# One 128-row product for the output of the later chunks of a gated linear attention with a mixing layer

## The chip, the cores and the metric

The kernel runs on one core of a Trainium2 chip. The metric is the device time of one execution in microseconds; the figure of a kernel is the median of its runs.

## What is computed

A gated linear attention over 4 batches of 8 heads, 768 positions and 48 channels a head, and behind it a mixing layer over the 384 joined channels. Everything is fp32. The change lies in the attention.

```
# attention
f = 1 / (1 + exp(-f_logit))
for t in range(S):
    state = f[:, :, t, :, None] * state + einsum('bhd,bhe->bhde', k[:, :, t], v[:, :, t])
    y[:, :, t] = einsum('bhd,bhde->bhe', q[:, :, t], state)
# mixing layer, x = y with its heads joined
theta = x @ w_theta
zr, zi = x * cos(theta), x * sin(theta)
u = x + einsum('ts,bsd->btd', w_tok_r, zr) + einsum('ts,bsd->btd', w_tok_i, zi)
out = u + max(u @ w_ch, 0)
```

## The kernel before

The positions of a batch are cut into 6 chunks of 128 (`NC`), so there are 24 chunks, `m` from 0 to 23. Heads are held in 4 pairs (`NP`): in a tile of q, k or f, rows 0 to 47 are the channels of the pair's first head and rows 64 to 111 those of its second, the columns are the pair and the position. The gates of a chunk are summed along the positions (`gate_sum`, a scan against the `carry` tile of ones and zeros), and q and k are scaled with their exponentials, so that within a chunk the attention is a masked product of q and k, and what came before is a state of 48x48 for each head.

A chunk is worked on in halves of 64 positions (`HALVES`, `t`), and `j` counts the two heads of a pair. Its steps:

- `sc` (`att_scores`): 16 matmuls make the key-value products of each half and head (line 312), and 16 the scores of the half against itself (line 318). Two of the four PSUM banks `a` receive them, one for each `j`. In the last chunk of a batch the second half's key-value products are left out.
- `sa` and `st` (`att_mid`, `att_new`) on VectorE add the products to the state: `mid` is the state at the chunk's middle, `st` at its end. `sm` fades it.
- `ma` (`att_mask`): two operations on VectorE multiply the scores with the `causal` triangle.
- `oa` (`att_old`, line 395): 16 matmuls of q with the state: the old state for the first half (none in the first chunk of a batch, so 8 matmuls there), `mid` for the second.
- `ob` (`att_own`, line 406): 16 matmuls of the masked scores with v, added to those of `oa` in PSUM.
- `xc` copies the result out, and the mixing layer takes it on.

All of these matmuls have at most 64 rows and 64 columns of weights. Scores of the pair's second head are written to the rows of the other half (`rows(j, t)`), and v is loaded with a second, rolled copy of the odd heads, so that the four matmuls of a group fall on the four different 64x64 tiles of the array. An fp32 matmul shows as two instructions in the trace.

The mixing layer runs on full 128x128 tiles with 384 columns: `th` (angles, 9 instructions), `f` (the products over positions, line 531, 6 instructions a step, or 4 in the first batch), `c` (the channel product, line 549, 9 a step). `tn`, `se`, `ab`, `tr`, `ro`, `zh`, `zl`, `v`, `uh`, `ul`, `cv` and `so` are its steps on the other engines. `fl` (line 583) is one product with a single column that sums up a flag.

There is no scheduler: `ORDER` is a table of some 1,200 step names, each calls its function once with the next number, and every engine runs its instructions in the order in which the steps stand there. A name after a slash sends a step to another engine (`/D` VectorE, `/A` ScalarE, `/P` GpSimd). `wu` steps at the start keep TensorE working on the `carry` tile while the first loads arrive. All loads are issued by SyncE, in that order, and each waits there until its buffer is free: `lf`, `lk`, `lq`, `lv` (line 600, two buffers) and `lw` for the weights.

Of the kernel before, what the change touches and what calls it, by code (L numbers as in the profile page):

```python
# [8 lines left out]
F32 = mybir.dt.float32  # L9
F32R = mybir.dt.float32r  # L10
I32 = mybir.dt.int32
U16 = mybir.dt.uint16
F16 = mybir.dt.float16
BF16 = mybir.dt.bfloat16
AF = mybir.ActivationFunctionType
ALU = mybir.AluOpType
# [6 lines left out]
P = 128  # L23
# [20 lines left out]
FULL = 1  # L44

CUT = 0
KB, XB = 10, 12
BL = 32

# [3 lines left out]


ORDER = (
# [36 lines left out]
)  # L92


# [1 line left out]
def gla_moe_kernel(  # L96
# [4 lines left out]
    f: bass.AP,  # L101
    v: bass.AP,
    vt: bass.AP,
    w_theta: bass.AP,
    w_r: bass.AP,
    w_i: bass.AP,
# [11 lines left out]

    carry = const.tile([P, NP, C], F32, tag="carry", name="carry")
    nc.vector.memset(carry, 1.0)
    nc.vector.memset(carry[:, :, 0:1], 0.0)

    causal = const.tile([P, C // 2], F32, tag="causal", name="causal")
    nc.gpsimd.memset(causal, 1.0)
# [143 lines left out]
    pss, scs, psks, kts, pkvs, mids, states, pys, xs, pxts = ({} for _ in range(10))  # L270
    HALVES = [(t, slice(64 * t, 64 * t + 64)) for t in range(2)]

    def rows(j, t):

        return HALVES[j ^ t][1]
# [28 lines left out]
    def att_scores(m):  # L304
        kt, qt = loaded["k", m], loaded["q", m]
        pss[m] = [bank([P, NP, C], f"pss{m}{j}", 1) for j in range(2)]
        pkvs[m] = [t[:, :, 64:64 + D] for t in pss[m]]
        for p in range(NP):
            for j, r in HALVES:
                h, c = 2 * p + j, slice(64 * j, 64 * j + D)  # L310
                for t, ts in HALVES[:1 if last_chunk(m) else 2]:
                    nc.tensor.matmul(pkvs[m][t][c, p, :], kts[m][ts, p, c], vs[m][ts, h * D:(h + 1) * D],  # L312
                                     start=True, stop=True)
        for p in range(NP):
            for t, ts in HALVES:
                for j in range(2):
                    r = slice(64 * j, 64 * j + D)
                    nc.tensor.matmul(pss[m][j][rows(j, t), p, :64], kt[r, p, ts], qt[r, p, ts], start=True, stop=True)  # L318

    def att_mask(m):  # L320
        t = sb.tile([P, 2, NP, C // 2], F32, tag="sc", bufs=2, name=f"sc{m}")
        scs[m] = [t[:, j] for j in range(2)]
        for j in range(2):
            masked = nc.vector.tensor_tensor(scs[m][j], pss[m][j][:, :, :64],  # L324
                                             causal.unsqueeze(1).to_broadcast([P, NP, 64]), op=ALU.mult)
            if not j:
                after(masked, old_done[m])
# [3 lines left out]
    def warm_up(n):  # L331

        if n < 4:
            nc.tensor.matmul(banks[n], carry[:, 0, :], carry.rearrange("p n t -> p (n t)"), start=True, stop=True)
            return
        nc.tensor.matmul(warm, carry[:, 0, :], carry[:, 1, :], start=True, stop=True)

    def att_keys(m):
        psks[m] = bank([P, NP, C], f"psk{m}", 1)
# [256 lines left out]
        return go  # L596

    def load_v(m):
        vs[m] = sb.tile([P, DM + NP * D], F32, tag="v", bufs=2, name=f"v{m}")
        nc.sync.dma_start(vs[m], v[m // NC, m % NC])  # L600

# [15 lines left out]
    def group(fn):  # L617
# [13 lines left out]
        "e4": lambda n: split_hi(NCH + n), "e5": lambda n: split_lo(NCH + n),  # L631
        "wu": warm_up, "gp": gate_end, "sa": att_mid,
        "sc": att_scores, "ma": att_mask, "ke": att_keys, "kt": att_ktok,
        "xb": x_turn, "xw": x_store, "xr": x_load,
        "kb": keys_turn, "ks": keys_store, "kl": keys_load,
        "st": inner(att_new), "sm": inner(att_fade), "oa": att_old, "ob": att_own, "xc": att_x, "xt": att_turn, "xs": keep_x,
# [101 lines left out]
def layout(inputs):  # L738
    import numpy as np

    def rows(a):
        t = np.asarray(a).transpose(0, 1, 3, 2).reshape(B, NP, 2, D, S)
        t = np.concatenate([t, t[:, :, :, :64 - D]], axis=3).reshape(B, NP, P, NC, C)
        return np.ascontiguousarray(t.transpose(0, 3, 2, 1, 4))

    v = np.asarray(inputs["v"])
    vc = v.transpose(0, 2, 1, 3).reshape(B, NC, C, NP, 2, D)
    odd = np.roll(vc[:, :, :, :, 1], C // 2, axis=2).reshape(B, NC, C, NP * D)
    vt = v.transpose(0, 1, 3, 2).reshape(B, NP, 2, D, S)
    vt = np.concatenate([vt, vt[:, :, :, :64 - D]], axis=3).reshape(B, NP, P, S)  # L750
    return {
# [2 lines left out]
        "f": rows(inputs["f_logit"]),  # L754
        "v": np.concatenate([vc.reshape(B, NC, C, DM), odd], axis=3),
        "vt": np.ascontiguousarray(vt),
        "w_theta": np.ascontiguousarray(inputs["moe_w_theta"]).view(np.int64),
        "w_r": np.ascontiguousarray(np.asarray(inputs["moe_w_tok_r"]).T).view(np.int64),
        "w_i": np.ascontiguousarray(np.asarray(inputs["moe_w_tok_i"]).T).view(np.int64),
# [22 lines left out]
```

## Time and profile before

| what | value |
|---|---|
| runs | 323.01, 324.25, 328.32 us; median 324.25 |
| the profiled execution's own time | 321.26 us |
| its span in the profile | 319.5 us |
| TensorE busy | 308.1 us (96%) |
| VectorE busy | 248.5 us (78%) |
| ScalarE busy | 194.6 us (61%) |
| GpSimd busy | 59.3 us (19%) |
| granted clock of TensorE | 1.0 |

The profile is of one execution. Matmuls are pipelined and overlap, and their ends are modelled, so the time from one matmul's start to the next says more than its duration. PE is TensorE, PEld its weight loads, DVE is VectorE, ACT ScalarE, POOL GpSimd, SP SyncE. The part of the span around the first 10 us is spent on the first loads and gates, while TensorE runs its warm-up products.

### The profile page before, as it was taken

To read this page: it belongs to the slowest core of one execution; us is meant where nothing else is said; L and a number is where in the kernel's file an instruction comes from. 1 tells how busy PE (TensorE), PEld (TensorE's weight loads), DVE (VectorE), ACT (ScalarE), POOL (GpSimd) and SP (SyncE) were. 2 spreads that over 40 slices of the span, in tenths; PEclk is the share of its full clock that TensorE was granted. 3 is DMA by queue.
4 is the path that set the end of the run, shared out by engine and by line. 5 is a ranking of instruction groups with operands and counts; after the bars stand their busy time and mean duration, and the time that the engine had idled before them with its cause. 6 is when DMAs were issued, how large, how long until landed. Compare 5 with 4: busy or idle time off the path is not lost.

```text
span 319.5 us, 10259 instructions
## 1 busy us (share of the span) xinstructions
PE 308.1 (96%) x4314; PEld 279.5 (87%) x4314; DVE 248.5 (78%) x449; ACT 194.6 (61%) x346; POOL 59.3 (19%) x74
## 2 busy tenths in 40 slices
PE   7889999999999999999999999999999999999993
PEld 4767677668999999998999999998999999999993
DVE  3999998999999999988968789789637476652122
ACT  6899897999998998885248670875151333111000
POOL 3124123354044520211030102103200000000000
PEclk9999999999999999999999999999999999999999
DMA  7999889974327685868778787955661431100002
GB/s 229 397 313 399 322 248 345 339 253 124 114 34 207 203 212 137 220 164 215 175 177 209 191 205 215 224 113 149 148 149 41 107 69 33 49 27 25 25 28 79
DMA packets 82610, 55.23 MB, mean 173 GB/s; under 512 B 51584, under 2 KB 66432, under 8 KB 82560
## 3 DMA queue, kind: packets, MB, share of 16 engines
q1 hardware_dynamic: 82416, 54.34, 58.8%
q8 instruction: 35, 0.57, 0.8%
q10 hardware_dynamic: 144, 0.20, 0.2%
q14 instruction: 15, 0.12, 0.1%
HBM read 43.77 MB, written 10.75 MB: 171 GB/s over the span
## 4 chain that ended last, share of the span: by engine, by line
PE 77%; DMA 11%; DVE 4%; ACT 3%; SPq 2%; issue 1%; DVEq 0%; ACTq 0%
PE pm L531 43%; PE pch L549 11%; PE a L475 9%; PE a L406 3%; DMA v<-in_v_dram 3%; PE a L395 3%; DMA ut<-xd 3%; PE a L318 3%; PE a L312 2%; DMA raw<-in_w_i_dram 2%; DMA out_dram<-ut 2%; DMA k<-in_k_dram 2%; PE a L341 1%; PE a L419 1%; SPq L595 1%
## 5 line engine op out<-in xcount | busy, mean ns | idle before, releaser
L531 PE MATMUL pm<-wp,z 128*128 128x384 f32 x756 | 142.4, 339 | 0.0
L531 PEld LDWEIGHTS pm<-wp,z 128*128 128x128 f32 x756 | 131.1, 188 | 1.0
L549 PE MATMUL pch<-uhl,wch 128*128 128x384 f32 x216 | 41.2, 338 | 0.0
L549 PEld LDWEIGHTS pch<-uhl,wch 128*128 128x128 f32 x216 | 37.5, 188 | 0.4
L260 POOL TENSOR_TENSOR q<-q,p 128x512 f32<-128x512 f32 x15 | 22.2, 1478 | 54.0 <-DMA q<-in_q_dram 37.8
L245 DVE TENSOR_TENSOR_SCAN f<-carry,f 128x512 f32<-128x512 f32 x24 | 29.1, 1211 | 3.5 <-ACT f L241 3.4
L475 PE MATMUL a<-wth,xh 128*128 128x384 f32 x144 | 30.1, 344 | 0.9 <-ACT ktok L149 0.3
L149 ACT CAST uhl<-ut 128x384 fp32r<-128x384 f32 x18 | 9.2, 511 | 31.5 <-DVE ut L535 31.5
L475 PEld LDWEIGHTS a<-wth,xh 128*128 128x128 f32 x144 | 24.7, 188 | 2.2 <-ACT xh L149 0.6
L531 PE MATMUL pm<-value,zf 128*128 128x384 f32 x72 | 25.3, 495 | 0.0
L563 DVE SCALAR_TENSOR_TENSOR ut<-pch,ut 128x384 f32<-128x384 f32 x24 | 13.1, 549 | 14.8 <-PE pch L549 14.8
L381 POOL TENSOR_TENSOR st<-st,pes 128x192 f32<-128x192 f32 x17 | 11.0, 645 | 71.3 <-DVE st L377 71.3
L265 DVE SCALAR_TENSOR_TENSOR k<-f,k 128x512 f32<-128x512 f32 x24 | 17.5, 729 | 5.4 <-ACT f L253 4.0
L324 DVE TENSOR_TENSOR sc<-a,causal 128x256 f32<-128x256 f32 x48 | 17.9, 415 | 3.9 <-PE a L395 3.7
L508 DVE TENSOR_TENSOR w<-w,x 128x768 f32<-128x768 f32 x18 | 17.1, 949 | 4.8 <-ACT w L501 4.8
L406 PEld LDWEIGHTS a<-v,sc 64*64 64x64 f32 x768 | 15.0, 134 | 5.8 <-issue 1.7
L240 ACT ACTIVATE f<-f 128x512 f32<-128x512 f32 x24 | 15.1, 629 | 7.4 <-DMA f<-in_f_dram 7.4
L531 PEld LDWEIGHTS pm<-value,zf 128*128 128x128 f32 x72 | 13.0, 190 | 7.5
L500 ACT ACTIVATE w<-w 128x384 f32<-128x384 f32 x24 | 12.6, 524 | 11.2 <-DVE w L495 10.9
L515 DVE TENSOR_TENSOR z<-w,z 128x768 fp32r<-128x768 f32 x18 | 18.2, 1010 | 1.5 <-ACT z L149 1.4
L252 ACT ACTIVATE p<-f 128x512 f32<-128x512 f32 x24 | 15.2, 632 | 6.7 <-POOL q L260 4.6
L535 DVE TENSOR_TENSOR ut<-pm,ut 128x384 f32<-128x384 f32 x24 | 13.1, 550 | 7.4 <-PE pm L531 7.3
(92 smaller groups left out, 527.5 us busy)
## 6 DMA issues: line engine op xcount, KB each, us to landing
v<-in_v_dram SPq DMA_DIRECT2D x24, 288.0 KB, 4.4
f<-in_f_dram SPq DMA_DIRECT2D x24, 256.0 KB, 4.1
q<-in_q_dram SPq DMA_DIRECT2D x24, 256.0 KB, 4.4
k<-in_k_dram SPq DMA_DIRECT2D x24, 256.0 KB, 4.7
raw<-in_w_r_dram SPq DMA_DIRECT2D x12, 383.8 KB, 5.9
raw<-in_w_i_dram SPq DMA_DIRECT2D x12, 383.8 KB, 6.5
out_dram<-ut SPq DMA_DIRECT2D x23, 192.0 KB, 2.5
kd<-kt SPq DMA_DIRECT2D x56, 64.0 KB, 2.8
```

The costliest lines, as they stand in the source:

```text
L240: nc.scalar.activation(ft, ft, AF.Exp, scale=-1.0, accum_out=odds[:, col:col + 1])
L245: nc.vector.tensor_tensor_scan(fl, carry[:, pairs(h)].rearrange("p n t -> p (n t)"), fl, 0.0, ALU.mult, ALU.add)
L252: nc.scalar.activation(ps_[m][:, pairs(h)], ft, AF.Exp, scale=-1.0)
L260: on(nc.vector).tensor_tensor(qt, qt, ps_[m][:, pairs(h)], op=ALU.mult)
L265: nc.vector.scalar_tensor_tensor(kt, loaded["f", m][:, pairs(h)], E_TOP, kt, op0=ALU.min, op1=ALU.mult)
L324: masked = nc.vector.tensor_tensor(scs[m][j], pss[m][j][:, :, :64], causal.unsqueeze(1).to_broadcast([P, NP, 64]), op=ALU.mult)
L406: nc.tensor.matmul(pys[m][j][ts, p, :], l, r, start=(old[t] is None and p == 0), stop=(p == NP - 1))
L475: nc.tensor.matmul(pths[m], l, r, start=(n == 0), stop=(n == len(ms) - 1))
L508: nc.vector.tensor_tensor(zfs[m] if full else w, w, xs[m].unsqueeze(1).to_broadcast([P, 2, DM]), op=ALU.mult)
L515: nc.vector.tensor_tensor(zs[m][:, 0], zfs.get(m, ws.get(m)), zs[m][:, 1], op=ALU.subtract)
L531: nc.tensor.matmul(pms[g, d], l, r, start=(s == 0 and i == 0), stop=(s == NC - 1 and i == len(ms) - 1))
L549: nc.tensor.matmul(pcs[g, d], l, r, start=(es[0] == 0 and n == 0), stop=(es[-1] == KD - 1 and n == len(ms) - 1))
```

## The change

From chunk 12 on (`KC = 12`), `oa` and `ob` are one step `oc` (`att_both`). For one half and one head the weights of its matmul hold, over 128 rows, the masked scores (64 rows) and q (48 rows at the other 64), and the moving operand holds v and, in the same rows as q, the state. Where 16 rows are left between, `v`'s tile has zeros from a new input `vh`. For it:

- `lv` loads two pieces into a `v` tile of two halves; the rolled copy of the odd heads is no longer used there.
- `qc` (`join_q`) copies q into the two `join` tiles on ScalarE, four copies a chunk, two where there is no old state.
- `m0` and `m1` (`join_old`, `join_mid`) copy the old and the middle state into the `v` tile on ScalarE, two copies each.
- `ma` writes the masked scores into the join tiles with four operations over 64 rows.
- the scores of both heads are written to the rows of their own half.
- the join tiles take the two buffers that the masked scores of two chunks had.

A chunk without an old state (12 and 18) has `k = 64` rows in the first half's product, one with it 112, and the second half's always 128. The tile shape goes by the rows: 64x64 for 64 rows, 128x64 for 112 and 128.

`carry` holds bytes now, and the warm-up products read a tile of ones instead. `ORDER` is written anew for all chunks: as many `f`, `th` and `c` steps, but other places, and other engines for some (`tn/D` 7 times, was 12; `xs/D` 3, was 8; `xc/D` 13, was 6; `gq/P` 17, was 15; `d5/P` 4, was 6; `uh/D` 8, was 6).

```diff
+U8 = mybir.dt.uint8
+KC = 12
 ORDER = (
-    "tr se so kb lf sm/P ab/A cv ks tr oa gp v gq/P sc ma ul f lq sa so ge ro ob cv oa zh ro so f lq xc",
+    "se c st m1 ro sm/P xh xs xl oc zh gk sc lv qc gs f lk xc kl kb ge lf th zl ks gp cv m0 d5/P ma ab/A",
...
-    carry = const.tile([P, NP, C], F32, tag="carry", name="carry")
-    nc.vector.memset(carry, 1.0)
-    nc.vector.memset(carry[:, :, 0:1], 0.0)
+    some = sb.tile([P, DM], F32, tag="x", bufs=3, name="some")
+    nc.vector.memset(some, 1.0)
+    carry = const.tile([P, NP, C], U8, tag="carry", name="carry")
+    nc.vector.memset(carry, 1)
+    nc.vector.memset(carry[:, :, 0:1], 0)
...
+    def v_half(m, t):
+        return vs[m][HALVES[t][1], t, :] if m >= KC else vs[m][HALVES[t][1], :DM]
...
                 for j in range(2):
                     r = slice(64 * j, 64 * j + D)
-                    nc.tensor.matmul(pss[m][j][rows(j, t), p, :64], kt[r, p, ts], qt[r, p, ts], start=True, stop=True)
+                    out_rows = ts if m >= KC else rows(j, t)
+                    nc.tensor.matmul(pss[m][j][out_rows, p, :64], kt[r, p, ts], qt[r, p, ts], start=True, stop=True)
+
+    joins = {}
+
+    def join_q(n):
+        m = KC + n
+        joins[m] = [sb.tile([P, NP, 2, 64], F32, tag="sc", bufs=2, name=f"join{m}{t}") for t in range(2)]
+        for t, ts in HALVES:
+            if t or m % NC:
+                w = 64 if t else D
+                for j in range(2):
+                    a, b = 64 - 64 * t, 64 * j
+                    nc.scalar.copy(joins[m][t][a:a + w, :, j, :], loaded["q", m][b:b + w, :, ts])
+
+    def join_state(m, t, state):
+        st = vs[m][:, t, :].rearrange("q (p j d) -> q p j d", p=NP, j=2)
+        for j in range(2):
+            a, b = 64 - 64 * t, 64 * j
+            nc.scalar.copy(st[a:a + D, :, j, :], state[b:b + D])
+
+    def join_mid(n):
+        join_state(KC + n, 1, mids[KC + n])
+
+    def join_old(n):
+        m = KC + n // (NC - 1) * NC + n % (NC - 1) + 1
+        join_state(m, 0, states[m - 1])
+
+    def att_both(n):
+        m = KC + n
+        pys[m] = pkvs[m]
+        for p in range(NP):
+            for j in range(2):
+                for t, ts in HALVES:
+                    k = P if t else 64 + D if m % NC else 64
+                    h = 2 * p + j
+                    nc.tensor.matmul(pys[m][j][ts, p, :], joins[m][t][:k, p, j, :], vs[m][:k, t, h * D:(h + 1) * D],
+                                     start=True, stop=True)
 
     def att_mask(m):
+        if m >= KC:
+            for j in range(2):
+                for t, ts in HALVES:
+                    nc.vector.tensor_tensor(joins[m][t][ts, :, j, :], pss[m][j][ts, :, :64],
+                                            causal[ts].unsqueeze(1).to_broadcast([64, NP, 64]), op=ALU.mult)
+            return
...
     def load_v(m):
+        if m >= KC:
+            vs[m] = sb.tile([P, 2, DM], F32, tag="v", bufs=2, name=f"v{m}")
+            for r, src in ((slice(0, 64), slice(0, 64)), (slice(D, P), slice(64, P + 64 - D))):
+                nc.sync.dma_start(vs[m][r, r.start // D, :], vh[m // NC, m % NC, src])
+            return
```

What TensorE runs at the end of chunk 12. Names are tiles with their numbers: `sc12` are masked scores, `v12` the values, `a0` to `a3` the PSUM banks, `pch` the channel product `c`. Before, behind the scores of chunk 13:

```order
L318 MATMUL a2_94<-q13_1831,k13_1711 64x64
L406 MATMUL a1_93<-v12_1926,sc12_2222 64x48 x2
L406 MATMUL a0_92<-v12_1926,sc12_2222 64x48 x2
L406 MATMUL a1_93<-v12_1926,sc12_2222 64x48 x2
L406 MATMUL a0_92<-v12_1926,sc12_2222 64x48 x2
L549 MATMUL pch12_2245<-uhl10_1723,wch1_87 128x384
```

Of the change, behind a channel product and ahead of the key-value products of chunk 13 (line 321); `join120` is chunk 12's first half, `join121` its second:

```order
L602 MATMUL pch11_2116<-uhl12_2038,wch1_89 128x384
L363 MATMUL a0_94<-v12_1880,join120_1956 64x48
L363 MATMUL a0_94<-v12_1880,join121_1957 64x48
L363 MATMUL a1_95<-v12_1880,join120_1956 64x48
L363 MATMUL a1_95<-v12_1880,join121_1957 64x48
L321 MATMUL a2_96<-v13_1969,ktok13_2056 48x48
```

The product of chunk 12 has moved from behind the scores of chunk 13 to ahead of its key-value products; both fences leave out rows of the same pattern (there are eight rows of `L406` and sixteen of `L363`), and the first half and the second now alternate.

What VectorE runs around the masks of chunk 12. Before, they stand far behind the state of the chunk; the rows from its middle state to its end state:

```order
L371 COPY mid12_2072<-a1_93 128x192
L508 TENSOR_TENSOR w9_1964<-w9_1964,x9_1688 128x768
L377 TENSOR_TENSOR st12_2094<-a0_92,mid12_2072 128x192
L149 CAST z9_2096<-w9_1964 128x768
```

Of the change, the four masks come ahead of the middle state:

```order
L370 TENSOR_TENSOR join120_1956<-a0_94,causal_72 64x4x64
L370 TENSOR_TENSOR join121_1957<-a0_94,causal_72 64x4x64
L370 TENSOR_TENSOR join120_1956<-a1_95,causal_72 64x4x64
L370 TENSOR_TENSOR join121_1957<-a1_95,causal_72 64x4x64
L424 COPY mid12_2102<-a0_94 128x192
L616 SCALAR_TENSOR_TENSOR ut1_742<-pch10_2076,ut1_742 128x384
L535 TENSOR_SCALAR w10_2109<-a2_96 128x384
L540 SCALAR_TENSOR_TENSOR w10_2109<-w10_2109,a2_96 128x384
L430 TENSOR_TENSOR st12_2126<-a1_95,mid12_2102 128x192
```

The masks have become four rows of 64 partitions and have moved ahead of `mid12`.

## Rows read from the trace of the kernel before

**Rows 1.** The page: busy time of each engine, and 40 equal slices.
```profile
PE 308.1 (96%) x4314; PEld 279.5 (87%) x4314; DVE 248.5 (78%) x449; ACT 194.6 (61%) x346; POOL 59.3 (19%) x74
DVE  3999998999999999988968789789637476652122
PEclk9999999999999999999999999999999999999999
```
**Rows 2.** Busy time by stretch; columns as the second row names them.
```profile
core 0: us, PE busy (x) PEld busy (x) DVE busy (x) ACT busy (x) POOL busy (x), PEclk, DMA share, GB/s
60.00:120.00 60.00, 59.87 (x894) 52.49 (x893) 58.86 (x98) 57.21 (x103) 23.71 (x20) 1.00 0.59 172
120.00:260.00 140.00, 138.77 (x2136) 132.35 (x2134) 111.89 (x212) 76.01 (x134) 18.24 (x25) 1.00 0.66 163
```
**Rows 3.** Waits of TensorE: who for whom, us in total, times, longest.
```profile
PE a L334 <- DVE carry L123: 1.8, 1, 1.8
PE a L312 <- issue: 0.8, 1, 0.8
```
**Rows 4.** Groups of instructions on TensorE, by shape: busy us, mean ns.
```profile
L406 PE MATMUL a<-v,sc 64*64 64x48 f32 x768 | 18.2, 222 | 0.0
L395 PE MATMUL a<-mid,q 48*64 48x48 f32 x384 | 15.9, 221 | 0.0
```
**Rows 5.** Timeline of TensorE, 178 to 187 us: start, us, instruction, count.
```profile
178.54 0.47 PE L312 MATMUL a<-v,ktok 64*48 64x48 f32 x13
178.82 0.27 PE L318 MATMUL a<-q,k 48*64 48x64 f32 x1
...
179.49 5.48 PE L531 MATMUL pm<-wp,z 128*128 128x384 f32 x30
184.90 0.68 PE L406 MATMUL a<-v,sc 64*64 64x48 f32 x32
185.40 0.22 PE L395 MATMUL a<-st,q 48*64 48x48 f32 x1
```
**Rows 6.** The same timeline, the end of that block.
```profile
185.97 4.44 PE L531 MATMUL pm<-wp,z 128*128 128x384 f32 x24
```
**Rows 7.** Timeline of TensorE, chunk 16's scores.
```profile
168.50 0.55 PE L312 MATMUL a<-v,ktok 64*48 64x48 f32 x32
168.87 0.67 PE L318 MATMUL a<-q,k 48*64 48x64 f32 x32
```
**Rows 8.** Timeline of TensorE, `oa` of chunk 12 and what follows it.
```profile
135.46 0.49 PE L395 MATMUL a<-mid,q 48*64 48x48 f32 x10
135.74 0.25 PE L312 MATMUL a<-v,ktok 64*48 64x48 f32 x2
```
**Rows 9.** Timeline of TensorE around the flag's product.
```profile
225.62 0.69 PE L475 MATMUL a<-wth,xl 128*128 128x384 f32 x3
226.23 0.19 PE L583 MATMUL a<-worst,pair 128*1 128x1 f32 x2
226.35 1.83 PE L549 MATMUL pch<-uhl,wch 128*128 128x384 f32 x9
228.03 1.23 PE L531 MATMUL pm<-wp,z 128*128 128x384 f32 x6
```
**Rows 10.** Timeline of TensorE, a long run of `f` steps.
```profile
283.16 7.46 PE L531 MATMUL pm<-wp,z 128*128 128x384 f32 x42
290.46 1.73 PE L549 MATMUL pch<-uhl,wch 128*128 128x384 f32 x9
```
**Rows 11.** Groups on VectorE and ScalarE, by shape: busy us, mean ns, idle before.
```profile
L149 ACT COPY x<-a 128x192 f32<-128x192 f32 x36 | 9.7, 319 | 6.4 <-PE a L406 6.2 <-DVE w L508 0.2
L324 DVE TENSOR_TENSOR sc<-a,causal 128x256 f32<-128x256 f32 x48 | 17.9, 415 | 3.9 <-PE a L395 3.7
L373 DVE TENSOR_TENSOR mid<-a,st 128x192 f32<-128x192 f32 x20 | 7.0, 349 | 2.9 <-PE a L318 2.6
L482 DVE TENSOR_SCALAR w<-a 128x384 f32<-128x384 f32 x12 | 6.6, 548 | 1.8 <-PE a L475 1.6
L149 DVE COPY ut<-a 128x384 f32<-128x384 f32 x8 | 4.4, 547 | 0.0
L149 DVE COPY x<-a 128x192 f32<-128x192 f32 x12 | 3.7, 351 | 1.0 <-PE a L406 1.0
```
**Rows 12.** Waits of the DMA queue on SyncE, the `v` loads.
```profile
SPq L600 <- PE a L406: 14.4, 8, 3.5
```
**Rows 13.** The `v` loads' line: ns of an issue, minimum, median, maximum.
```profile
L600 SPq DMA_DIRECT2D v<-in_v_dram x24: 327/384/1011, 4.2 to 249.0; - x24
```

More of the change, by code (lines that the diff above doesn't have):

```diff
@@ L103, in gla_moe_kernel @@
     vt: bass.AP,
+    vh: bass.AP,
     w_theta: bass.AP,
@@ L311, in att_scores @@
                 for t, ts in HALVES[:1 if last_chunk(m) else 2]:
-                    nc.tensor.matmul(pkvs[m][t][c, p, :], kts[m][ts, p, c], vs[m][ts, h * D:(h + 1) * D],
+                    nc.tensor.matmul(pkvs[m][t][c, p, :], kts[m][ts, p, c], v_half(m, t)[:, h * D:(h + 1) * D],
                                      start=True, stop=True)
@@ L333, in warm_up @@
         if n < 4:
-            nc.tensor.matmul(banks[n], carry[:, 0, :], carry.rearrange("p n t -> p (n t)"), start=True, stop=True)
+            nc.tensor.matmul(banks[n].rearrange("p (n t) -> p n t", n=NP), some[:, :C],
+                             some[:, :C].unsqueeze(1).to_broadcast([P, NP, C]), start=True, stop=True)
             return
-        nc.tensor.matmul(warm, carry[:, 0, :], carry[:, 1, :], start=True, stop=True)
+        nc.tensor.matmul(warm, some[:, :C], some[:, C:2 * C], start=True, stop=True)
     def att_keys(m):
@@ L633, in gla_moe_kernel @@
         "sc": att_scores, "ma": att_mask, "ke": att_keys, "kt": att_ktok,
+        "qc": join_q, "m0": join_old, "m1": join_mid, "oc": att_both,
         "xb": x_turn, "xw": x_store, "xr": x_load,
@@ L748, in layout @@
     odd = np.roll(vc[:, :, :, :, 1], C // 2, axis=2).reshape(B, NC, C, NP * D)
+    vr = vc.reshape(B, NC, C, DM)
     vt = v.transpose(0, 1, 3, 2).reshape(B, NP, 2, D, S)
@@ L756, in layout @@
         "vt": np.ascontiguousarray(vt),
+        "vh": np.concatenate([vr[:, :, :C // 2], np.zeros_like(vr[:, :, :64 - D]), vr[:, :, C // 2:]], axis=2),
         "w_theta": np.ascontiguousarray(inputs["moe_w_theta"]).view(np.int64),
```

71 rows, old and new, of the table ORDER are left out of this document.

## The prediction

> **What bounds the kernel now.** First the page's busy times and slices [rows 1]: TensorE is busy for 308.1 of 319.5 us at the full granted clock (every PEclk digit is 9). The stretches [rows 2] divide this. From 60 to 120 us TensorE, VectorE and ScalarE are all full (59.87, 58.86 and 57.21 of 60). From 120 us, where the second half of the chunks is worked on, VectorE has 28 us free of 140 and ScalarE 64, while TensorE has 1.2. The waits of TensorE [rows 3] are short: 1.8 us for the first warm-up operand, then none over 0.8. So a change to TensorE's work after 120 us moves the end one for one, and extra work on the other two engines there has cover; before 120 us the three are level, and only the order has changed there.
>
> A busy TensorE isn't TensorE at its peak, so its prices are taken from starts. A long run of `f` steps starts 42 instructions in 7.30 us, 0.174 us each [rows 10]. The 64-row products stand in the profile with a mean of 220 ns and overlap [rows 4]: 32 instructions (16 fp32 matmuls, two instructions each) of `ob` start in 0.50 us, from 184.90 to 185.40, 15.6 ns each [rows 5], with four tiles of 64x64 in use.
>
> **Does half the matmuls mean half the time?** The old tile has 64 rows and 64 columns, so four fit. The new one has 128 rows and 64 columns, so two fit. The trace has places where only two tiles are in use. In chunk 12 there is no old state, so `oa` uses the second half's columns alone: ten instructions start from 135.46 to 135.74, 28 ns each [rows 8]. In chunk 17, the last of its batch, the key-value products use the first 64 rows alone, with both column halves: 13 in 0.28 us, 21.5 ns each [rows 5], where chunk 16 with four tiles starts 32 in 0.37 us, 11.6 ns each [rows 7]. With half the tiles each instruction takes 1.8 times as long. So 32 instructions of `oc` take 32 x 28 ns = 0.90 us, nearly what `oa` and `ob` take together. Bounds: 15.6 ns if the count of instructions set the pace (0.50 us), 56 ns if only one tile at a time made progress (1.8 us). I take 28 ns, the row with 64 columns of weights and two tiles. Over twelve chunks: before 10 x 0.50 + 2 x 0.45 (`oa`, 16 instructions of 28 ns in chunks 12 and 18) + 12 x 0.50 = 11.9 us; after 12 x 0.90 = 10.8. **-1.1 us.**
>
> **Trips between tile shapes.** From 179.49 to 185.97 there are 30 `f` instructions, `ob` and `oa` [rows 5, 6]: 6.48 us, less 30 x 0.174 and 2 x 0.50, leaves 0.27 us for going from 128x128 tiles to the small ones and back, 0.135 a switch. It is not the overlap with small rows alone: the flag's product L583, 128 rows by one column between full products, is a trip too. From 225.62 to 228.03 stand 3 + 9 full instructions and its two: 2.41 - 12 x 0.174 = 0.32 us [rows 9]. Counted in `ORDER` from `sc` of chunk 12 on, there were 16 such trips; now there are 13: **-0.8 us.** But `oc` has a shape of its own (128x64) beside `sc` (64x64), and eleven times one follows the other within a trip: 11 x 0.135 = **+1.5 us** (bounds 0 and 3.0, a whole trip each).
>
> **Chunks 12 and 18.** The order above shows their sixteen matmuls alternating between join0 and join1. Without an old state the first half's product has 64 rows (`k = 64`) and the second's 128, so the tile shape changes at every matmul. One visit of two instructions costs, by L583, 0.12 us from its start to that of the next shape [rows 9]; a 64-column operand adds one tile period (2 x 28 = 56 ns) and the stream of 48 columns some 0.03 (48/384 of 0.174, once or twice). That is 0.21 us a visit, 16 visits 3.4 us instead of 0.90: 2.5 us more in each of the two chunks, **+5.0 us.** No row shows a switch between 64x64 and 128x64, and these two tiles share no columns, so 0 is the other bound; 0.32 x 16 in place of 0.90, twice, is 8.4. I take 5.0, since every change of shape that the trace shows costs a trip, with few rows or all. The Trainium skill, TensorEngine Tiling, section Tiling Modes, says that changing the mode, and not only the tile, drains the engine; by it the alternation costs as I take it, and the trace agrees as far as it has such changes (0.27 and 0.32 us a trip).
>
> **The other engines.** VectorE gets four masks of 64 rows for two of 128. A mask has 256 elements a row in either form and takes 415 ns [rows 11], so 24 more are 10 us. ScalarE gets 44 pairs of small copies, 88 of some 0.32 us (the x copies of 192 elements, [rows 11]): 28 us. VectorE's 28 us and ScalarE's 64 free us after 120 [rows 2] cover both. The cover is thinnest near chunks 12 to 14, where VectorE is nearly full, but there `oc` of chunk 12 gives VectorE 2.5 us. Cost 0, up to 2.5 if the three chunks' six extra masks there stand before work that TensorE waits for. The narrowest distance from a chunk's `sc` to its `oc` in the new order is that of chunk 23, five `f` steps of six instructions, 5.2 us; behind `sc` the middle state (0.35), its copies (2 x 0.32) and four masks (1.7) need under 3 [rows 11]. SyncE issues twelve more v loads at 0.38 us [rows 13]; their buffer now is freed by `oc` where it was by `ob` (14.4 us of waits on that queue already, hidden; [rows 12]). Cost 0 to 1, taken 0. The byte-sized carry, warm-up operand and moved steps before chunk 12 change no duration that a row shows; five `tn` and five `xs` leave VectorE (10 x 0.55 us), seven `xc` of two copies come to it (14 x 0.35), near even [rows 11]. Taken 0, from -2 to +2, since three level engines leave an order little to gain.
>
> **Sum.** -1.1 - 0.8 + 1.5 + 5.0 = +4.6 us on the profiled 321.26, so 325.9. That execution is 3.0 below the median of the runs, 324.25; on the median it is 328.9, 1.4% more.
>
> **Rivals.**
> - *The engine does not stop between tiles that share no columns.* The alternation is free and, with the switch beside `sc` kept, the sum is -0.4: 323.9; with that free too, -1.9: 322.4. For it: chunk 17's two column halves run side by side [rows 5]. Against: rows 9. This is the side on which the kernel is no slower; it decides when a visit costs under 0.08 us. Chance 0.25.
> - *The count of instructions sets the pace.* `oc` takes 0.50: 4.8 us less, 317.6 with the alternation and the switches free. Against: the two-tile rows 5 and 8. Chance 0.05.
> - *Weights over all rows load one after the other.* Each instruction takes a tile period alone, 56 ns: 0.9 us more in ten chunks, 328.9 + 9 = 337.9. Against it: one tile's period is the same with both column halves on one group of rows (2 x 21.5 ns, [rows 5]) as with four tiles (4 x 11.6, [rows 7]), so two loads on the same rows do not queue. The Trainium skill, TensorE: Matmul & The Clock Gate, Part 3, says that a weight load overlaps running matmuls only where the row group differs, which `oc` never has. The trace disagrees for 64 rows (those 43 and 46 ns) and shows nothing for 128 rows by 64 columns. Chance 0.07.
> - *The masks and joins come late.* VectorE's 10 us meet its full stretches before 150 us and TensorE waits: 2.5 to 4 us more, 332. For it: VectorE's slices of 9 up to the middle of the span [rows 1]. Chance 0.13.
> - *The forecast.* 0.50.
>
> **Numbers.** 328.9 us. The first rival must be in and the fourth up to its larger part: 321.5 to 333.0, which leaves out the second, the third and little else; the forecast's own range is 326 to 331.5. Two per cent, about what a measurement here can tell from no change, lies at 317.8 and 330.7. Faster by more: the second rival, 0.05. Slower by more: the third 0.07, most of the fourth 0.10 and the upper end of the forecast 0.10, together 0.27. Within: 0.68.
>
> **What would show it.** In the changed profile the sixteen `oc` matmuls of chunks 13 to 17 and 19 to 23 should start 32 instructions in 0.9 us, and those of chunks 12 and 18 in 3 to 4 us. If chunk 12 takes 0.9 us too, the first rival holds. If an ordinary `oc` takes 0.5 or 1.8 us, the second or third does. If TensorE shows waits for masks, joins or v after 120 us of more than 2 us in sum, the fourth. A gain or loss before 120 us of over 2 us would prove the order's share wrong.

## The result and the profile after

| | kernel before | changed kernel |
|---|---|---|
| median of 20 runs each, on the same chip | 324.49 us | 327.87 us |
| lowest and highest | 320.25, 329.28 | 325.03, 333.90 |
| ratio, 95% interval | | 1.0133 (1.0108 to 1.0158) |
| profiled execution | 321.26 us | 328.53 us |

The ratio leaves out of either kernel the runs over 1.5% above its fastest (the slow state; three of the changed kernel's twenty), so it is not the quotient of the two medians. The changed kernel is 1.3% slower, 4.3 us on 324.25. The first lines of its page answer to [rows 1]:

```profile
span 326.8 us, 9689 instructions
PE 315.0 (96%) x3962; PEld 285.2 (87%) x3962; DVE 261.0 (80%) x479; ACT 223.9 (69%) x426; POOL 57.4 (18%) x73
PEclk9999999999999999999999999799999999999998
```

TensorE has 352 instructions fewer and is busy 6.9 us longer; the rest of the span, 11.8 us, is what it was (11.4). One digit of the granted clock is a 7 (and the last, where TensorE's work is over, an 8), where before all were 9. By stretch, beside [rows 2]:

```profile
core 0: us, PE busy (x) PEld busy (x) DVE busy (x) ACT busy (x) POOL busy (x), PEclk, DMA share, GB/s
60.00:120.00 60.00, 59.33 (x916) 51.21 (x915) 58.48 (x99) 55.58 (x99) 19.50 (x17) 1.00 0.60 167
120.00:260.00 140.00, 140.00 (x1652) 133.52 (x1652) 117.30 (x227) 101.33 (x206) 19.70 (x27) 0.99 0.66 156
136.10:140.00 3.90, 3.90 (x82) 3.81 (x81) 3.02 (x8) 3.76 (x10) 1.21 (x2) 1.00 0.58 155
201.40:205.30 3.90, 3.90 (x33) 3.03 (x32) 3.33 (x6) 1.53 (x4) 0.00 (x0) 1.00 0.58 172
205.60:209.00 3.40, 3.40 (x65) 3.28 (x56) 2.15 (x4) 2.03 (x4) 0.00 (x0) 0.50 0.41 110
```

From 120 to 260 us TensorE shows no idle time at all (it had 1.2 us before), VectorE has 5 us more work and ScalarE 25 us more, and both still have room. The added time lies inside TensorE's own work. The timeline says in which:

```profile
132.23 3.96 PE L363 MATMUL a<-v,join 64*64 64x48 f32 x32
136.13 0.57 PE L321 MATMUL a<-v,ktok 64*48 64x48 f32 x32
...
201.41 3.96 PE L363 MATMUL a<-v,join 64*64 64x48 f32 x32
205.31 0.73 PE L321 MATMUL a<-v,ktok 64*48 64x48 f32 x32
205.81 1.11 PE L328 MATMUL a<-q,k 48*64 48x64 f32 x32
206.85 3.32 PE L584 MATMUL pm<-wp,z 128*128 128x384 f32 x12
210.01 1.20 PE L528 MATMUL a<-wth,xh 128*128 128x384 f32 x6
...
229.57 0.57 PE L321 MATMUL a<-v,ktok 64*48 64x48 f32 x32
229.97 0.66 PE L328 MATMUL a<-q,k 48*64 48x64 f32 x32
230.56 1.14 PE L363 MATMUL a<-v,join 112*64 112x48 f32 x32
231.63 0.62 PE L584 MATMUL pm<-wp,z 128*128 128x384 f32 x2
```

L363 is `oc`; a row names its run of instructions by the first of them. In chunks 12 and 18 (the first two) `oc` holds the engine for 3.90 us, from its start to that of the next work. In the others, of which the last block is one, it is 1.07 us, the switch to the next shape included. And behind chunk 18 comes the low digit: at 205.60 the granted clock is 0.50, the lower level of 1.2 GHz, for some 3.4 us, after 3.9 us in which the shape changed at every matmul. The scores there take 1.54 us (205.31 to 206.85) where the last block has 0.99, and twelve `f` instructions 3.16 where [rows 10] give 2.09: 1.6 us lost. Behind chunk 12 the clock stayed at 1.0 (the stretch from 136.10).

The waits of TensorE, beside [rows 3], show none for a mask or a join:

```profile
PE a L386 <- DVE some L126: 1.5, 1, 1.5
PE a L321 <- DMA v<-in_v_dram: 1.3, 2, 0.7
PE a L448 <- DVE st L430: 1.1, 3, 0.5
```

And the groups that the change adds or enlarges, beside [rows 11]:

```profile
L370 DVE TENSOR_TENSOR join<-a,causal 64x256 f32<-64x256 f32 x48 | 20.1, 418 | 2.0 <-PE a L363 0.9 <-PE a L328 0.5
L340 ACT COPY join<-q 64x256 f32<-64x256 f32 x24 | 9.7, 405 | 0.3
L340 ACT COPY join<-q 48x256 f32<-48x256 f32 x20 | 8.1, 404 | 8.9 <-PE a L363 8.6
L346 ACT COPY v<-mid 48x192 f32<-48x192 f32 x24 | 8.4, 349 | 1.6 <-DVE mid L426 1.2
L346 ACT COPY v<-st 48x192 f32<-48x192 f32 x20 | 7.0, 351 | 0.4
```

### The profile page after: what moved, and what is told of

The parts are those of the page before. It is cut to its first block, busy times and chain, and to the rows that moved or that the text cites. A ratio compares the mean times of both kernels' runs of the same rounds, so it can differ in the third digit from the quotient of the medians.

```text
span 326.8 us, 9689 instructions
## 1 busy us (share of the span) xinstructions
PE 315.0 (96%) x3962; PEld 285.2 (87%) x3962; DVE 261.0 (80%) x479; ACT 223.9 (69%) x426; POOL 57.4 (18%) x73
## 4 chain that ended last, share of the span: by engine, by line
PE 86%; DMA 8%; DVE 3%; issue 0%; ACT 0%; SPq 0%; DVEq 0%
PE pm L584 45%; PE pch L602 12%; PE a L528 10%; PE a L363 6%; DMA raw<-in_w_i_dram 4%; PE a L321 3%; PE a L328 3%; DMA raw<-in_w_r_dram 2%; PE a L386 2%; DMA v<-in_v_dram 2%; PE a L459 1%; PE a L448 1%; PE a L394 1%; PE a L472 1%; PE warm L389 1%; DVE f L251 1%
## 5 line engine op out<-in xcount | busy, mean ns | idle before, releaser
L266 POOL TENSOR_TENSOR q<-q,p 128x512 f32<-128x512 f32 x17 | 23.2, 1366 | 56.5 <-PE a L363 17.3
L251 DVE TENSOR_TENSOR_SCAN f<-carry,f 128x512 f32<-128x512 uint8 x24 | 30.1, 1259 | 3.0 <-ACT f L247 3.0
L155 ACT CAST uhl<-ut 128x384 fp32r<-128x384 f32 x16 | 8.0, 511 | 31.9 <-DVE ut L588 31.9
L340 ACT COPY join<-q 64x256 f32<-64x256 f32 (+1 forms) x44 | 17.8, 404 | 9.2 <-PE a L363 8.6
L434 POOL TENSOR_TENSOR st<-st,pes 128x192 f32<-128x192 f32 x17 | 12.0, 709 | 65.6 <-DVE st L430 65.6
L588 DVE TENSOR_TENSOR ut<-pm,ut 128x384 f32<-128x384 f32 x24 | 13.1, 551 | 12.8 <-PE pm L584 12.7
L370 DVE TENSOR_TENSOR join<-a,causal 64x256 f32<-64x256 f32 x48 | 20.1, 418 | 2.0 <-PE a L363 0.9
L262 POOL COPY pes<-p 128x4 f32<-128x4 f32 x24 | 11.7, 488 | 55.1 <-ACT p L258 55.1
L363 PEld LDWEIGHTS a<-v,join 128*64 128x64 f32 (+2 forms) x384 | 16.2, 137 | 3.9 <-issue 2.0
L363 PE MATMUL a<-v,join 128*64 128x48 f32 (+2 forms) x384 | 19.3, 226 | 0.0
```

What stands on the lines that cost most here:

```text
L251: nc.vector.tensor_tensor_scan(fl, carry[:, pairs(h)].rearrange("p n t -> p (n t)"), fl, 0.0, ALU.mult, ALU.add)
L266: on(nc.vector).tensor_tensor(qt, qt, ps_[m][:, pairs(h)], op=ALU.mult)
L340: nc.scalar.copy(joins[m][t][a:a + w, :, j, :], loaded["q", m][b:b + w, :, ts])
L363: nc.tensor.matmul(pys[m][j][ts, p, :], joins[m][t][:k, p, j, :], vs[m][:k, t, h * D:(h + 1) * D], start=True, stop=True)
L370: nc.vector.tensor_tensor(joins[m][t][ts, :, j, :], pss[m][j][ts, :, :64], causal[ts].unsqueeze(1).to_broadcast([64, NP, 64]), op=ALU.mult)
```

## The experiments

**One shape in chunks 12 and 18.** The theory: the alternation of shapes is the loss. The rival: the loss lies elsewhere in the change (copies, order, the 128-row product). This kernel keeps the change and pads the missing old state with zeros, so that all sixteen matmuls use 128x64 tiles.

```
+        if m % NC == 0:
+            nc.gpsimd.memset(vs[m][64:64 + D, 0, :], 0.0)
...
-            if t or m % NC:
+            if True:
...
-                    k = P if t else 64 + D if m % NC else 64
+                    k = P if t else 64 + D
```

> The changed kernel with one thing undone: chunks 12 and 18 get 112 rows in their first half too (q is copied there as in other chunks, the state's rows are filled with zeros), so their sixteen products no longer change the tile shape from one to the next. Theory (a change of shape stops the engine): both take 1.07 us like the other chunks instead of 3.89, 5.7 us less, and the 3.4 us at half the granted clock that followed chunk 18 go too, some 1.5 us: about 321 us, a ratio to the kernel before of 0.990 to 0.996. Rival (the loss is in the new order, before chunk 12 and in waits): the two products get shorter but the ratio stays above 1.008.

Measured: 322.59 us, ratio to the kernel before 1.0015 (0.9981 to 1.0049). Its timeline at chunk 12 and its stretch:

```profile
131.17 1.14 PE L365 MATMUL a<-v,join 112*64 112x48 f32 x32
132.24 0.57 PE L321 MATMUL a<-v,ktok 64*48 64x48 f32 x32
```

```profile
core 0 of [0], span 319.6 us
120.00:260.00 140.00, 138.75 (x1740) 132.63 (x1739) 122.44 (x239) 105.71 (x216) 19.88 (x28) 1.00 0.65 156
```

`oc` of chunk 12 is down from 3.90 to 1.07 us with the same number of matmuls (the first half's now over 112 rows), and no stretch has a lower clock until TensorE's work is over. From there on TensorE does the same work in the same order in both kernels: from this `oc`'s start to the end of the span it is 326.8 - 132.23 = 194.6 us with the alternation and 319.6 - 131.17 = 188.4 without. The 6.1 us compare with 2 x 2.83 for the two products and 1.6 for the clock, together 7.3, so 1.1 came back elsewhere. The two timelines show where: behind chunk 17 the padded kernel, 2.8 us ahead by then, stands 0.86 us for ScalarE's cast of `xh`, which the next angles are made from, and the kernel with the alternation does not.

```profile
185.25 5.48 PE L586 MATMUL pm<-wp,z 128*128 128x384 f32 x30
191.59 1.32 PE L530 MATMUL a<-wth,xh 128*128 128x384 f32 x6 [0.86 <-ACT xh L155]
```

From the first row to the second it is 6.34 us here and 5.35 in the changed kernel (189.07 to 194.42), 1.0 us of the 1.1. The ratios differ by 0.0118 +/- 0.004, 3.8 +/- 1.4 us over the runs, so the profiled pair stands rather above the middle. The alternation is the loss; that the rest of the change then makes the kernel faster, as the theory had it (0.990 to 0.996), isn't seen.

**Two more chunks with alternation.** Chunks 13 and 14 get it too (the rows of their old state are left out).

```
-                    k = P if t else 64 + D if m % NC else 64
+                    k = P if t else 64 + D if m % NC and m not in (13, 14) else 64
```

> The changed kernel with the same alternation in two more chunks: 13 and 14 leave the old state out of their first half (64 rows). Theory: each takes 3.9 us instead of 1.07, 5.7 us more in sum, ratio to the kernel before 1.030, and up to 1.040 if the granted clock falls behind each. Rival (chunks 12 and 18 are slow for another reason, as what they wait for): under 1 us more, ratio 1.013 to 1.016.

Measured: 337.71 us, ratio 1.0436 (1.0342 to 1.0529). Chunk 13, and three stretches (columns as above) of the profiled execution, which at 339.49 us is the longest of the four:

```profile
147.23 3.96 PE L363 MATMUL a<-v,join 64*64 64x48 f32 x32
151.12 0.57 PE L321 MATMUL a<-v,ktok 64*48 64x48 f32 x32
```

```profile
135.00:142.00 7.00, 7.00 (x85) 6.65 (x84) 4.29 (x10) 4.53 (x11) 2.46 (x3) 0.52 0.56 146
166.00:169.00 3.00, 3.00 (x11) 2.82 (x12) 2.55 (x6) 2.48 (x7) 0.00 (x0) 0.50 0.74 149
213.00:220.00 7.00, 7.00 (x90) 6.27 (x90) 3.81 (x7) 2.44 (x5) 0.00 (x0) 0.55 0.40 121
```

Chunk 13's `oc` takes 3.89 us, as in chunk 12 of the changed kernel, though it holds an ordinary chunk's data. The two added alternations cost 0.030 of ratio, 9.8 +/- 3.1 us, where their own price makes 2 x 2.8; the upper end of what was expected is passed. The stretches show where more can come from: the granted clock is at its lower level at the end of three of the four alternations and behind them (chunks 12, 14 and 18, not 13), for some 17 us in all, against 3.4 us in the changed kernel's profile. The other three executions agree: their mean granted clock is 0.972 to 0.987, where that of the seventeen runs in the changed kernel's ratio is 0.987 to 0.996. So chunk 13 shows the same direct price as chunk 12, and the clock's share comes on top and varies.

**The same matmuls, sorted.** In chunks 12 and 18 the eight matmuls of the first half come first and then the eight of the second, so that the shape changes once.

```
+        every = [(p, j, t) for p in range(NP) for j in range(2) for t in range(2)]
+        if m % NC == 0:
+            every.sort(key=lambda i: i[2])
```

> The changed kernel with the sixteen products of chunks 12 and 18 in another order: first the eight of 64 rows, then the eight of 128, one change of shape within instead of fifteen. Theory: 32 instructions on one tile at a time, 56 ns each, and one switch, 2.0 us instead of 3.89; 3.8 us less in sum, and less of the low clock: ratio to the kernel before 0.996 to 1.002. Rival (64-row products are slow among 128-row ones whatever the order): 3.9 us stays, ratio 1.013.

Measured: 323.34 us, ratio 1.003 (0.9982 to 1.0078), a little above what the theory gave, with its range inside the interval.

```profile
134.44 2.19 PE L366 MATMUL a<-v,join 64*64 64x48 f32 x32
136.56 0.57 PE L321 MATMUL a<-v,ktok 64*48 64x48 f32 x32
```

`oc` of chunk 12 takes 2.12 us: each half now uses a single tile, which by the prediction's 56 ns makes 32 x 56 ns = 1.8 us, and there are two switches. Nothing but the order of sixteen matmuls in two chunks differs from the changed kernel, and 0.010 of ratio, 3.3 +/- 1.8 us, is gone, beside 2 x 1.78 us less on TensorE. This rules out that the 64 rows, the missing copy or the data are the cause of these 1.78 us.

**The kernel before, once more.** In the changed profile TensorE was behind before chunk 12 already. The kernel before starts that chunk's first product at 135.46 us [rows 8] and has done 33 full instructions (24 of `f`, 9 of `th`) more by then, 5.7 us; without them it would stand at 129.7. The changed kernel starts `oc` at 132.23, 2.5 us later. Is that the new order?

```
(no edit)
```

> The kernel before, unchanged, for a second profile. The first channel product of batch 0's second half (c, line 549, the step numbered 3) started at 126.5 us in the first profile; by its amount of work on TensorE the changed kernel stood 2.5 us later there. Theory that this is the order's: it starts at 126 to 127 again. Rival (it differs from run to run): 128 to 129.

Measured: 321.96 us. The same channel product of the same kernel, in the first profile and in this one:

```profile
126.47 1.73 PE L549 MATMUL pch<-uhl,wch 128*128 128x384 f32 x9
```

```profile
128.12 1.73 PE L549 MATMUL pch<-uhl,wch 128*128 128x384 f32 x9
```

Two executions of one kernel differ by 1.65 us at this place. By the second, the changed kernel is 0.9 us behind and not 2.5; what is left is less than the difference between the two, so no share of the loss can be given to the order before chunk 12. A loss there of a microsecond or two isn't excluded either. Six profiles have the new order and the same work on TensorE up to chunk 12; its `oc` starts at 132.23 (changed), 131.17 (padded), 131.83 (two more alternations), 134.44 (sorted), 131.92 and 132.69 us (two and four tiles, below), where the kernel before would stand at 129.7 and 131.4.

**All matmuls 64 rows, on two tiles.** `k = 64` everywhere: the other rows' products are left out. This removes every change of shape between `sc` and `oc` and tests whether 128 rows are dearer than 64.

```
-                    k = P if t else 64 + D if m % NC else 64
+                    k = 64
```

> The changed kernel with 64 rows in every product of oc, those of the masked scores in the first half and of q in the second, so that what stands in the other rows is left out. All are 64x64 tiles on the same 64 rows, two tiles in use, and the shape is that of sc. Theory (tiles in use set the pace, a change of shape costs about 0.13 us): 32 instructions start in 0.93 to 0.97 us in every chunk, where the changed kernel shows 1.07, and chunks 12 and 18 are like the rest. Rival (128 rows slow each instruction): well under 0.9 us.

Measured: 320.01 us in a single run. The same block as the last one of the timeline above:

```profile
221.70 0.57 PE L321 MATMUL a<-v,ktok 64*48 64x48 f32 x32
222.09 0.66 PE L328 MATMUL a<-q,k 48*64 48x64 f32 x32
222.57 1.09 PE L363 MATMUL a<-v,join 64*64 64x48 f32 x32
223.60 1.14 PE L584 MATMUL pm<-wp,z 128*128 128x384 f32 x5
```

From the first product to the first `f` it is 1.90 us, against 2.06 with 128 rows: the one switch from 64x64 to 128x64 costs up to 0.16 us. `oc` itself is 1.03 us with its switch to the full tiles, against 1.07: half the rows make it hardly cheaper. In chunk 12, where the shape does not change behind it, it is 0.9:

```profile
131.92 1.08 PE L363 MATMUL a<-v,join 64*64 64x48 f32 x30
132.81 0.25 PE L321 MATMUL a<-v,ktok 64*48 64x48 f32 x2
```

In chunks 14 and 17 it is 1.20 and 1.26, so the 0.93 to 0.97 that were expected do not hold in every chunk.

**The same on four tiles.** As before, with the zeros and the copies of q of the first experiment kept, but the matmuls of the pair's second head take the other 64 rows, so that the four tiles of the array are in use (again only one part of each product is made).

```
...
-                    k = P if t else 64 + D if m % NC else 64
+                    z = slice(64, 64 + D) if (j, t) == (1, 0) else rows(j, t)
...
-                    nc.tensor.matmul(pys[m][j][ts, p, :], joins[m][t][:k, p, j, :], vs[m][:k, t, h * D:(h + 1) * D],
+                    nc.tensor.matmul(pys[m][j][ts, p, :], joins[m][t][z, p, j, :], vs[m][z, t, h * D:(h + 1) * D],
```

> The same with 64 rows, but those of the pair's second head come from the other group of 64 rows, so that the four products of a group lie on four tiles; again half of the rows are left out. Number of instructions, columns and shape are those of the run with two tiles. Theory (tiles in use): 0.47 to 0.50 us for 32 instructions, 0.57 less in each of twelve chunks than the padded kernel, and since TensorE is the bound 6 to 7 us less in all: ratio to the kernel before 0.978 to 0.986. Rival (some other engine takes over as the bound): 0.5 us each in the profile, but a ratio over 0.992.

Measured: 318.48 us, ratio 0.9819 (0.9746 to 0.9891).

```profile
239.74 0.68 PE L365 MATMUL a<-v,join 64*64 64x48 f32 x32
240.24 0.56 PE L321 MATMUL a<-v,ktok 64*48 64x48 f32 x32
```

32 instructions start in 0.50 us, the pace of `ob` before [rows 5]. The count of matmuls is that of `oc`; only the number of tiles in use has changed, and the time falls from 0.9 us (chunk 12 on two tiles) to little over half. Not every chunk has it: over the twelve, `oc` takes 7.1 us here and 12.8 in the padded kernel, 5.8 less and not 12 x 0.57 = 6.8. Chunks 14 and 17 take 0.95 and 0.87. In chunk 14 the product starts before VectorE is done with its masks:

```profile
153.26 1.73 DVE L372 TENSOR_TENSOR join<-a,causal 64x256 f32<-64x256 f32 x4
...
154.78 1.02 PE L365 MATMUL a<-v,join 64*64 64x48 f32 x32
```

The ratio falls by 0.020, 6.4 +/- 2.6 us. In the profiles 4.5 of the 5.8 us arrive (from chunk 12's `oc` to the end 316.6 - 132.69 = 183.9 us, against 188.4 padded); behind chunk 17 TensorE now stands 1.22 us for the cast of `xh`. So most of what TensorE gains here arrives at the end, but not one for one.

**The carry in bytes alone.** The kernel before with the byte-sized `carry` and the new warm-up operand, since the scan reads 1259 ns in the changed profile where it was 1211.

```
-    carry = const.tile([P, NP, C], F32, tag="carry", name="carry")
+    carry = const.tile([P, NP, C], mybir.dt.uint8, tag="carry", name="carry")
...
-        nc.tensor.matmul(warm, carry[:, 0, :], carry[:, 1, :], start=True, stop=True)
+        nc.tensor.matmul(warm, some[:, :C], some[:, C:2 * C], start=True, stop=True)
```

> The kernel before with one part of the change alone: the carry tile of the gate scans holds bytes, and the warm-up products read a tile of ones. The scan takes 1259 ns with bytes in the changed kernel's profile, 1211 before. Theory (this is the bytes' price, mostly hidden): 1247 to 1260 ns here too, 1.1 us more on VectorE in all, ratio to the kernel before 0.998 to 1.005. Rival (the longer scans stem from what runs beside them): 1211 ns.

Measured: 323.27 us, ratio 0.9942 (0.9894 to 0.999).

```profile
L247 DVE TENSOR_TENSOR_SCAN f<-carry,f 128x512 f32<-128x512 uint8 x24 | 29.2, 1216 | 3.1 <-ACT f L243 3.1
```

The scan with bytes takes 1216 ns, nearly as with fp32 (1211), so the rival holds. What makes it 48 ns longer in the changed kernel was not found. The half per cent of gain is below what the theory gave, 1 only just lies outside its interval, and its cause is open.

**The change in the old order.** The padded kernel, with the table of the kernel before: `oa` dropped from chunk 12 on, `oc` in `ob`'s place, and the copies put in by hand, `qc` ahead of `ma`, `m1` behind `sa`, `m0` behind the new state. One row of the table of before and what it became:

```
-kl d5/P xl lv go th gk ab/A zl f lf cv tn f xs/D so kb c gs ks tr se f ro oa cv go sc lq ma zh/D ob
+kl d5/P xl lv m0 go th gk ab/A zl f lf cv tn f xs/D so kb c gs ks tr se f ro cv go sc lq qc ma zh/D oc
```

> The one product in the old order: the table of the kernel before, with oa dropped, oc in the place of ob, the copies of q ahead of the masks and those of the states behind the additions that make them; chunks 12 and 18 padded. The masks of several chunks stand a few steps ahead of their product there. Theory (the order is there to hide the copies and masks): TensorE waits 1 to 2 us in several chunks, 4 to 10 us more in all: ratio 1.012 to 1.03. Rival (the distances are enough in the old order too): 0.996 to 1.006, as the padded kernel in the new order.

Measured: 354.01 us, ratio 1.0868 (1.0754 to 1.0982), far beyond what either theory gave.

```profile
SPq L650 <- ACT join L342: 34.1, 7, 9.2
```

```profile
ACT v L348 <- DVE mid L426: 13.0, 2, 12.6
...
PE a L365 <- ACT join L342: 4.1, 8, 0.7
```

```profile
200.00:240.00 40.00, 32.72 (x340) 30.55 (x339) 25.70 (x52) 22.20 (x44) 4.12 (x7) 0.83 0.61 143
```

These are of the longest of the four executions, 358.16 us; the last row has the columns as above. No engine is full here: TensorE works 32.7 us of 40. The copy of q comes right before the product that needs it, so TensorE waits for it, and the next load of q (L650) waits on its queue for 34 us in all until the copies have read the old one; the loads behind it on SyncE wait with it. On ScalarE the copies of the state stand up to 12.6 us for VectorE's `mid`, with the mixing layer's work queued behind. The granted clock is 0.83 in this stretch. This placement of the copies was mine, and an earlier one in the old table was not tried; shown is only that these copies and that table together cost 9%, where the same copies in the new table cost nothing that can be seen.

## Why the prediction was right

It said 328.9 us and "within 2%", by a loss of 4.6 us on TensorE; measured were 327.87 us and a ratio that makes 4.3 us of loss. The mechanism is shown, but that the two figures lie 0.3 us apart is in part luck: the alternation was put 0.7 us too low and the clock not at all, and against both stands a part of TensorE's loss that does not reach the end. Step by step:

- **Half the matmuls, the same time: right.** 32 instructions of `oc` were put at 0.90 us from chunk 12's `oa` [rows 8]. They take 1.07 with a switch of 0.16 or less, so 0.91 or a little more. The run on four tiles gives 0.50 for the same count, so tiles in use set the pace. This refutes the second rival (the count of instructions) and the third, by which it would be 1.8: 128 rows cost as much as 64, within 0.04 us. The Trainium skill, TensorE: Matmul & The Clock Gate, Part 3, says that a weight load overlaps running matmuls only where the row group differs, and all of `oc` use the same. By that rule, with one tile's period of 56 ns, `oc` would take some 1.8 us (an estimate); the trace disagrees, with 1.07.
- **The switch between `sc` and `oc`: right.** 0.135 us was taken from trips that the trace had; up to 0.16 was measured.
- **Alternation in chunks 12 and 18: right in kind, a little small.** 0.21 us a visit was put together from the flag's product [rows 9]; it is 3.90 / 16 = 0.24. The two products cost 3.90 us each instead of 3.4, so the term was 2 x 2.83 = 5.7 and not 5.0. The padded kernel, the two added alternations and the sorted order all show it, and with them the first rival falls: the engine does stop between tiles that share no columns. The Trainium skill, TensorEngine Tiling, section Tiling Modes, says that a change of mode drains the engine; the trace agrees.
- **Not foreseen: the clock.** Each alternation keeps TensorE at 32 small instructions in 3.9 us, and behind one of the two the granted clock fell to 0.50, for 1.6 us of loss in the profile. The sum has no such term. The mean granted clock says that this is no single case: in the runs that the ratios are taken from it is 0.991 for the changed kernel and 0.995 for the padded one (both with the idle end of the span in it). Over the runs less than products and clock together is lost: with the alternation undone 3.8 +/- 1.4 us come back, which holds the 5.0 of the sum but not the 5.7 of the two products, still less 7.3 with the clock.
- **One for one: not quite.** The prediction lets every change of TensorE's work after 120 us reach the end whole. In the profiled pair 6.1 of 7.3 us do, since the padded kernel, further ahead, stands 0.86 us for a cast behind chunk 17; of the gain on four tiles 4.5 of 5.8 us do. What lies between the 6.1 us of the pair and the 3.8 of the runs is open.
- **The other engines: right.** The masks took 418 ns where 415 was put; the copies 33 us in all where 28 was put, since a copy of q takes 0.40 and not 0.32. All of it is hidden: no wait of TensorE for masks or joins shows up, so the fourth rival falls. The cover is thin: on four tiles, where TensorE comes earlier, chunk 14's product meets masks that are not done. The run in the old order shows that it also depends on where the copies stand.
- **Trips and order: small, as put, but not separated.** Without the alternation the sum was -0.4 us; measured are 0.5 +/- 1.1. By the profiles the changed kernel is 2.5 us behind at chunk 12 beside the first profile of before and 0.9 beside the second, and loses 4.8 or 5.7 us from there on, where the sum has 4.6. The loss of over 2 us that was to prove the order's share wrong so shows beside one profile and not beside the other, and this share stays open.

No kernel here with the one product, and with the whole of it, is better than the kernel before: the padded one equals it within its interval, and the kernels on two and four tiles that were quicker leave half of the rows out. One product over 128 rows has little to win here, since the two products that it replaces ran on four tiles.

## What to carry to other kernels

Count the tiles in use, not the matmuls: one product over twice the rows on two tiles takes about as long (0.9 us) as two products on four (2 x 0.50). Keep one tile shape within a group of matmuls; where one operand is shorter, padding it with zeros cost nothing that showed, and leaving the rows out in every second matmul cost 2.8 us for sixteen of them. Work that is moved to an idle engine has to stand early enough that neither the consumer nor the next load of its source waits for it; in the run in the old order both did.

## What was not expected of the hardware

After 3.9 us of alternating shapes, in which the profile shows TensorE busy throughout, the granted clock can fall to its lower level: for 3.4 us behind one of two alternations in the changed kernel's profile, for some 17 us in all in that with four. A busy share of 1.00 does not say that the engine is working at its rate: in these 3.9 us it starts 32 small instructions that take 1.07 us without the alternation. In the sorted kernel, which has no alternation, the same fall is seen once early, after TensorE was busy for 3.19 us of 5; its longest stop there, 1.25 us, the profile puts down to no other engine:

```profile
20.00:25.00 5.00, 3.19 (x103) 2.25 (x102) 3.63 (x6) 3.68 (x8) 1.45 (x3) 1.00 0.96 348
25.00:31.00 6.00, 5.80 (x74) 5.18 (x75) 4.02 (x10) 4.07 (x6) 2.29 (x3) 0.50 0.81 312
```

The scan on VectorE takes 1211 and 1212 ns with an fp32 constant in the two profiles of the kernel before, and with one of bytes 1216 to 1300 ns from kernel to kernel, with operands of the same size; as it is 1216 with the bytes alone, what makes it longer is open.
